# Gated GELU projection on one core: eight early units instead of six, with their first blocks loaded in sequence of columns

## The chip, the cores and the metric

The kernel runs on one core of one Trainium2 chip. A core has TensorE (matrix products, accumulated in eight PSUM banks of 128 x 512 float32), VectorE and ScalarE (which read SBUF and PSUM), GpSimd (SBUF only) and SyncE, which here issues DMAs. In the profile they are PE (PEld is its weight load), DVE, ACT, POOL and SP. The metric is the device time of one execution in microseconds (us); of several executions the median counts.

## The reference

```python
def reference(x, w_gate, w_up, w_down):
    g = jnp.einsum("bsd,df->bsf", x, w_gate)
    u = jnp.einsum("bsd,df->bsf", x, w_up)
    h = _gelu(g) * u
    return jnp.einsum("bsf,fd->bsd", h, w_down)
```

x is 2048 x 1024, w_gate and w_up are 1024 x 3584, w_down is 3584 x 1024, all bf16. `_gelu` is the tanh approximation. The output is 2048 x 1024.

## The kernel before

**Passes and units.** The 2048 rows of x are taken in two passes of 1024 (`ip`), each in two halves c = 0 and 1 of 512 rows. In SBUF, x stands transposed as `xT[c]`: 128 partitions of the contraction index, eight K blocks of 128 (four "lo", four "hi"), 512 rows. The 3584 columns of w_gate and w_up are 28 blocks of 128. A *unit* (`unit`, line 222) computes two blocks h = 0 and 1 of h = gelu(g) * u for both halves c, in a scheme of seven products instead of eight: the 2 x 2 matrix of (block, K half) times the 2 x 2 matrix of (K half, row half). Its operands are sums. `sums_t` (line 149) makes t1 to t4 out of the four quarters of x, once a pass, four 128 x 512 sums each, and `tb` as a cast. `sums_s` (line 164) makes s1 to s4 out of the four quarters of a unit's weights, two 128 x 512 sums each (gate and up), and `sa` as a cast. The products are

- P1 = a11 b11 and P2 = a12 b21, of plain bf16 data, whose sum is the result for block h = 0 and c = 0;
- s2 t2 (on top of P1), s1 t1, s3 t3, s4 tb and sa t4, of the sums in float32.

Each has eight matmuls of 128 x 128 by 128 x 512: four K blocks for gate and four for up. A unit's P1 and P2 are thus 16 matmuls in bf16, and the five others 40. P1 is copied from PSUM to SBUF by ScalarE (`snap`, line 106) before P2 is added in the same bank. Between the products ScalarE copies partial results (u2, p5), takes gelu, and VectorE adds and multiplies; the finished block goes to `hT`.

**Early units.** In the first pass the first R = 6 units have P1 and P2 done ahead of all float32 products, because those need nothing but x and the first block of the unit's weights. `early_p1`, `early_snap`, `early_p2` and `early_c11` (lines 503 to 524) do this; `seed` (line 526) later puts P1 back into PSUM. The units from R on have P1 and P2 done in `raw_products`, two units at a time, ahead of the last product of an odd unit (`ahead_of_p4`, line 621). Which blocks of columns early units take is free; `block` (line 139) says where they stand in `hT`.

**Weights.** `load_w` (line 124) loads 256 columns (rows of 512 bytes) of w_gate and of w_up, 512 KB each, so one load holds two blocks. Later units use the two blocks of one load. The early units use two loads together: units 0 and 1 take their first blocks from load 0 and their second ones from load 1, units 2 and 3 from loads 2 and 3, units 4 and 5 from loads 4 and 5. Loads 0 to 2 stand in the three buffers of `wpool`, loads 3 to 5 in the part of `hT` that is written last.

**What sets the order.** VectorE, GpSimd, SyncE and TensorE run their instructions in the order of the source. ScalarE's order comes from the framework's scheduler and departs from the source in places. Each engine works its list strictly in order and waits for semaphores. SyncE's list is the order of the loads (lines 482 to 496); load 4 alone is issued by ScalarE (line 553). The second half of x is transposed by two DMAs (line 490), the first by TensorE (`turn`, line 457) from plain loads.

**The stage in question** (lines 530 to 573): the first rows of x are turned while P1 of units 0 and 1 starts; P2 of these; P1 and P2 of units 2 and 3; the same for units 4 and 5. On VectorE stand in between t1, s1, s2 of unit 0, then t2, t3, s3, s4 and t4. GpSimd makes the sums of unit 1 (`make_s(early[1], pool)`, line 573) and then, inside each unit (`prepare`, line 603), those of the next one, with nothing ahead of them but the loads. `pool_behind` (line 179) is defined and not used: a one-element copy on GpSimd that waits for a given tile.

**After the units** the second projection (`down`, line 372) runs with a similar scheme over `hT`; the second pass follows. Neither is touched.

Of the kernel before, what the change touches and what calls it, by code (L numbers as in the profile page):

```python
# [10 lines left out]
def kernel(  # L11
# [39 lines left out]
    NKB = Dm // P  # L51
# [3 lines left out]
    N = 512  # L55
# [1 line left out]
    NPASS = S // (2 * N)  # L57
    NU = NFB // 2
    NWARM = 7
    R = 6  # L60
    SLOTS = 52
    LAG = 3
    BIG12 = (0, 2, 4)
# [47 lines left out]
    def as_f32(ap):  # L111
        return ap.rearrange("p a b -> p (a b)").bitcast(f32)

    def matmul(ps, lhs, rhs, start, stop):
        nc.tensor.matmul(  # L115
            ps, lhsT=lhs, rhs=rhs, start=start, stop=stop, skip_group_check=True
        )
# [3 lines left out]
    def new_w():  # L121
        return wpool.tile([P, 2, NKB, 2 * P], bf16, name="w")

    def load_w(n, w, k0=0, k1=NKB, queue=nc.sync):
        f0 = n * 2 * P
        for i, src in enumerate((w_gate, w_up)):
            queue.dma_start(  # L127
                out=w[:, i, k0:k1],
                in_=src[k0 * P : k1 * P, f0 : f0 + 2 * P].rearrange(
                    "(ko ki) f -> ki ko f", ki=P  # L130
                ),
            )
        return w

    def blocks_of(w, w2=None, q=0):
        pair = ((w, 0), (w, 1)) if w2 is None else ((w, q), (w2, q))
        return [[v[:, i, :, n * P : (n + 1) * P] for i in range(2)] for v, n in pair]

    def block(ip, u, h):
        return u // 2 * 4 + 2 * h + u % 2 if ip == 0 and u < R else 2 * u + h  # L140

    class Sums(dict):

# [328 lines left out]
    def transposing(xT, c, ko, r0):  # L472
# [2 lines left out]
        )  # L475

    on_dve, on_act = nc.vector.tensor_copy, nc.scalar.copy
    far = hT[:, 1, 2:14].rearrange("p j c n -> p (j c n)").rearrange(
        "p (m i k f) -> p m i k f", m=3, i=2, k=NKB
    )  # L480
    wa = {0: new_w(), 1: new_w(), 2: new_w(), 3: far[:, 0], 4: far[:, 1], 5: far[:, 2]}
    load_x(0)
    load_w(0, wa[0], 0, 2)
    load_w(0, wa[0], 2, 4)
    load_x(1)
    load_w(0, wa[0], 4, 8)
    load_w(2, wa[2])
    for half in range(2):
        ks = slice(half * KH, (half + 1) * KH)
        nc.sync.dma_start_transpose(  # L490
            out=xT[1][:, ks], in_=x2[N : 2 * N, half * N : (half + 1) * N]
        )
        if half == 0:
            load_w(1, wa[1])
    load_w(3, wa[3])
    load_w(5, wa[5])
    early = [blocks_of(wa[u // 2 * 2], wa[u // 2 * 2 + 1], u % 2) for u in range(R)]
    seen = xpool.tile([P, 1], f32, name="seen")
    E, K, C, F = odd, cc, dd, even
    s, t = sums_s(early[0], dve), sums_t(xT)  # L500
    p1s = {}

    def early_p1(u, ps, i, ks, cols=slice(0, N)):
        for k in ks:
            matmul(
                ps[i][:, cols],
                early[u][0][i][:, k, :],
                xT[0][:, k, cols],
                k == 0 and cols.start == 0,
                k == KH - 1,  # L510
            )

    def early_p2(u, ps, i, ks):
        for k in ks:
            matmul(ps[i], early[u][0][i][:, KH + k, :], xT[0][:, KH + k, :], False, k == KH - 1)

    def early_snap(u, ps):
        at = [None, None]
        if u >= 4:
            at = [as_f32(hT[:, n // 14, n % 14]) for n in (4 + 2 * u, 5 + 2 * u)]  # L520
        p1s[u] = [snap(ps[i], "p1", at[i]) for i in range(2)]

    def early_c11(u, ps):
        times(block(0, u, 0), 0, gelu(ps[0]), ps[1])

    def seed(u, e):
        for i in range(2):
            nc.scalar.copy(out=e[i], in_=p1s[u][i])  # L528

    on_queue = nc.scalar  # L530
# [50 lines left out]
    def loaded(u):  # L581
        if u not in ws:
            ws[u] = load_w(u, new_w())
        return blocks_of(ws[u])

    def raw_of(u, e):
        p1 = raw_products(e, K, xT, loaded(u))
        return lambda: finish_raw(2 * u, K, p1)

    def weights(ip, u):  # L590
        return early[u] if ip == 0 and u < R else loaded(u)

    for ip in range(NPASS):
        with tc.manual_schedule(engines={ENG.Activation}):
# [102 lines left out]
```

## Time and profile before

| | us |
|---|---|
| median of 3 runs (550.7 to 555.04) | 552.34 |
| the profiled execution | 551.14 |
| its span | 549.4 |
| TensorE busy, share of the span | 534.5, 97% |
| VectorE busy | 345.1, 63% |
| ScalarE busy | 271.0, 49% |
| GpSimd busy | 250.1, 46% |
| granted TensorE clock | 0.999 |

The span is from the first to the last instruction of the profiled execution. A line of the timeline gives the start and the time of a run of like instructions (us), the engine (SPq is SyncE's DMA issue), the source line, the operation, the tile written and those read, the shapes and the count, and in brackets how long the engine had been idle before and what ended the idle time. L115 is the helper for all matmuls, L91 and L94 those for two-operand operations on VectorE and GpSimd, L127 the weight loads. The chain of work that ended last is followed back from the last instruction, at each step to what released it; it is shown in order of time. TensorE's busy time is modelled at the ends of matmuls, so 97% does not mean that it is at its peak.

By stages (us of the span): up to 11.63 the first transposes and the P1 of units 0 and 1; to 22.33 their P2 and units 2 and 3; to 33.33 units 4 and 5; to 48.28 unit 0; then unit 1 to 57.51 and unit 2 to 66.74. DMAs move 260 GB/s from 3.60 to 33.33 and almost nothing from 34 to 46.

### The profile page before, as it was taken

The page shows a single profiled execution, that of the slowest core. Times are in us where ns is not written, and L with a number is a line of the kernel's source. Part 1 is how long each engine was busy: PE and PEld are TensorE (multiplying, and loading weights), DVE is VectorE, ACT ScalarE, POOL GpSimd, SP SyncE. Part 2 cuts the span into 40 slices and gives each one's busy share as a digit, 9 for nine tenths or more (in the row PEclk, how much of TensorE's full clock was granted, in tenths as well). Part 3 has the DMA queues.
Part 4 walks back from the last instruction along what each step waited for, and adds up shares of the span by engine and source line. Part 5 has one row for each costly group of instructions (what it writes and reads, how often), then busy time and mean ns, then how long its engine had stood idle before and what let it go on. Part 6 is the DMA issues. An engine that isn't in the chain of part 4 may idle for free.

```text
span 549.4 us, 7452 instructions
## 1 busy us (share of the span) xinstructions
PE 534.5 (97%) x2380; PEld 383.2 (70%) x2399; DVE 345.1 (63%) x520; ACT 271.0 (49%) x484; POOL 250.1 (46%) x220
## 2 busy tenths in 40 slices
PE   8878999999999999999999999999999999999997
PEld 4346787768686854888868686767768685478886
DVE  1596767667667696586874645555555548766730
ACT  3465786666675701155435564565555551114531
POOL 0369999767666310000058667676767600000000
PEclk9999999999999999999999999999999999999999
DMA  8951369394863799999937222222422039663751
GB/s 234 248 130 38 98 196 280 100 284 124 223 170 99 267 343 383 276 237 233 343 112 180 78 76 78 77 78 76 106 59 68 1 102 382 224 228 95 222 189 53
DMA packets 108520, 93.29 MB, mean 170 GB/s; under 512 B 17089, under 2 KB 93889, under 8 KB 108481
## 3 DMA queue, kind: packets, MB, share of 16 engines
q1 hardware_dynamic: 106400, 91.77, 57.3%
q10 hardware_dynamic: 2080, 1.05, 0.9%
q8 instruction: 19, 0.31, 0.2%
q14 instruction: 21, 0.16, 0.1%
HBM read 74.45 MB, written 15.20 MB: 163 GB/s over the span
## 4 chain that ended last, share of the span: by engine, by line
PE 88%; DMA 5%; DVE 3%; SPq 2%; issue 1%; ACT 0%; DVEq 0%; ACTq 0%
PE bank L115 88%; DMA raw<-in_w_down_dram 3%; DVE t L91 2%; DMA w<-in_w_up_dram 2%; SPq L127 1%; SPq L490 1%; DVE hT L91 1%; DVE s L91 0%; SPq L450 0%; ACT g L194 0%; DVE sum L91 0%; ACT st L419 0%; ACT bank L528 0%; DVEq L91 0%; SPq L340 0%
## 5 line engine op out<-in xcount | busy, mean ns | idle before, releaser
L94 POOL TENSOR_TENSOR s<-w 128x512 fp32r<-128x512 bf16 x88 | 103.2, 1190 | 169.4 <-DVE t L91 86.2
L115 PE MATMUL bank<-t,s 128*128 128x512 f32 x672 | 158.6, 391 | 4.8 <-ACT bank L528 2.3
L115 PEld LDWEIGHTS bank<-t,s 128*128 128x128 f32 x672 | 125.5, 188 | 33.9 <-POOL s L94 1.9
L115 PE MATMUL bank<-xT,w 128*128 128x512 bf16 (+1 forms) x411 | 90.2, 375 | 2.1 <-ACT p L108 1.2
L91 DVE TENSOR_TENSOR hT<-g,bank 128x512 bf16<-128x512 f32 x112 | 76.9, 688 | 22.4 <-PE bank L115 7.6
L194 ACT ACTIVATE g<-sum 128x512 f32<-128x512 f32 x78 | 49.5, 634 | 75.4 <-DVE sum L91 74.0
L108 ACT COPY p<-bank 128x512 f32<-128x512 f32 x96 | 54.3, 590 | 45.6 <-PE bank L115 45.3
L115 PEld LDWEIGHTS <-w 128*128 128x128 bf16 x424 | 40.3, 98 | 50.0 <-issue 4.4
L91 DVE TENSOR_TENSOR sum<-bank,p 128x512 f32<-128x512 f32 x36 | 24.9, 692 | 77.8 <-PE bank L115 77.8
L115 PE MATMUL bank<-q 128*128 128x512 f32 x240 | 58.9, 389 | 0.0
L115 PE MATMUL bank<-t,sa 128*128 128x512 f32 x224 | 57.6, 399 | 0.8 <-DVE sum L91 0.8
L94 POOL TENSOR_TENSOR s<-w,s 128x512 fp32r<-128x512 bf16 x48 | 56.0, 1187 | 0.0
L94 POOL TENSOR_TENSOR s<-s,w 128x512 fp32r<-128x512 f32 x48 | 55.7, 1182 | 0.0
L115 PE MATMUL bank<-tb,s 128*128 128x512 f32 x224 | 55.3, 389 | 0.0
L115 PEld LDWEIGHTS bank<-q 128*128 128x128 f32 x240 | 45.0, 188 | 9.4
L115 PEld LDWEIGHTS bank<-t,sa 128*128 128x128 f32 x224 | 42.0, 188 | 10.8 <-DVE sum L91 1.3
L115 PE MATMUL bank<-raw,hT 128*128 128x512 bf16 x218 | 48.5, 379 | 0.4
L103 ACT CAST tb<-raw 128x512 fp32r<-128x512 bf16 x28 | 17.3, 626 | 63.3 <-DMA raw<-in_w_down_dram 27.7
L115 PEld LDWEIGHTS <-hT 128*128 128x128 bf16 x256 | 24.7, 98 | 33.6 <-DMA hT<-in_w_up_dram 2.2
L115 PEld LDWEIGHTS bank<-tb,s 128*128 128x128 f32 x224 | 42.0, 188 | 8.7
L91 DVE TENSOR_TENSOR q<-hT 128x512 fp32r<-128x512 bf16 x56 | 38.4, 686 | 3.9 <-PE bank L115 3.9
L108 ACT COPY xT<-bank 128x512 f32<-128x512 f32 x56 | 31.5, 590 | 11.4 <-PE bank L115 6.2
(54 smaller groups left out, 543.5 us busy)
## 6 DMA issues: line engine op xcount, KB each, us to landing
raw<-in_w_down_dram SPq DMA_DIRECT2D x76, 256.0 KB, 4.8
q<-td SPq DMA_DIRECT2D x60, 256.0 KB, 5.0
w<-in_w_gate_dram SPq DMA_DIRECT2D x24, 512.0 KB, 5.4
w<-in_w_up_dram SPq DMA_DIRECT2D x24, 512.0 KB, 6.5
td<-m SPq DMA_DIRECT2D x12, 768.0 KB, 4.5
w<-td SPq DMA_DIRECT2D x6, 1024.0 KB, 10.3
out_dram<-st SPq DMA_DIRECT2D x32, 128.0 KB, 1.7
td<-w SPq DMA_DIRECT2D x2, 768.0 KB, 6.4
```

The source lines that it names most:

```text
L91: nc.vector.tensor_tensor(out=out, in0=a, in1=b, op=op)
L94: nc.gpsimd.tensor_tensor(out=out, in0=a, in1=b, op=op)
L103: nc.scalar.copy(out=t, in_=src)
L108: nc.scalar.copy(out=t, in_=ps)
L115: nc.tensor.matmul(ps, lhsT=lhs, rhs=rhs, start=start, stop=stop, skip_group_check=True)
L127: queue.dma_start(out=w[:, i, k0:k1], in_=src[k0 * P : k1 * P, f0 : f0 + 2 * P].rearrange("(ko ki) f -> ki ko f", ki=P),)
L194: nc.scalar.activation(g, src, ACT.Gelu_apprx_tanh)
L490: nc.sync.dma_start_transpose(out=xT[1][:, ks], in_=x2[N : 2 * N, half * N : (half + 1) * N])
```

## The change

R goes from 6 to 8. The first blocks of the eight early units are now the first eight blocks of columns: blocks 0 and 1 in `wa`, blocks 2 to 5 in `mid`, loaded with 512 columns (rows of 1 KB) in two K halves, blocks 6 and 7 in `end`. The second blocks come from loads 4 to 7: loads 4 and 5 at the start, loads 6 and 7 when `early(u)` first asks for them. `mid` and `end` stand in `hT`. All loads are on SyncE's queue, in the order x, `wa`, first half of `mid`, a transposed half of x, second half of `mid`, the other transposed half, `end`, load 4, load 5. P1 of units 2 to 5 now goes in one run, then their P2, then units 6 and 7. One of P1's two copies goes to the place in `hT` of the unit's second block. VectorE has t1 to t4 among the products of the early units and s1 to s4 behind them; `tb` is cast later; the last transposed block of x is copied by VectorE alone, and unit 0's P1 copies come earlier. A `pool_behind` on s2 of unit 0 stands ahead of GpSimd's sums of unit 1.

```diff
-    R = 6
+    R = 8
...
-    def load_w(n, w, k0=0, k1=NKB, queue=nc.sync):
+    def load_w(n, w, k0=0, k1=NKB, wide=2):
         f0 = n * 2 * P
         for i, src in enumerate((w_gate, w_up)):
-            queue.dma_start(
+            nc.sync.dma_start(
                 out=w[:, i, k0:k1],
-                in_=src[k0 * P : k1 * P, f0 : f0 + 2 * P].rearrange(
+                in_=src[k0 * P : k1 * P, f0 : f0 + wide * P].rearrange(
...
     def block(ip, u, h):
-        return u // 2 * 4 + 2 * h + u % 2 if ip == 0 and u < R else 2 * u + h
+        return u + R * h if ip == 0 and u < R else 2 * u + h
...
-    wa = {0: new_w(), 1: new_w(), 2: new_w(), 3: far[:, 0], 4: far[:, 1], 5: far[:, 2]}
+    far = hT[:, 1, 2:14].rearrange("p j c n -> p (j c n)")
+    wa, mid, end = new_w(), *[
+        v.rearrange("p (i k f) -> p i k f", i=2, k=NKB)
+        for v in (far[:, : 4 * NKB * 2 * P], far[:, 4 * NKB * 2 * P :])
+    ]
+    pairs_of = {0: new_w(), 1: new_w()}
+
+    def load_x1(half):
+        nc.sync.dma_start_transpose(
+            out=xT[1][:, half * KH : (half + 1) * KH],
+            in_=x2[N : 2 * N, half * N : (half + 1) * N],
+        )
+
     load_x(0)
-    load_w(0, wa[0], 0, 2)
-    load_w(0, wa[0], 2, 4)
+    load_w(0, wa, 0, 2)
+    load_w(0, wa, 2, 4)
     load_x(1)
-    load_w(0, wa[0], 4, 8)
-    load_w(2, wa[2])
-    for half in range(2):
-        ks = slice(half * KH, (half + 1) * KH)
-        nc.sync.dma_start_transpose(
-            out=xT[1][:, ks], in_=x2[N : 2 * N, half * N : (half + 1) * N]
-        )
-        if half == 0:
-            load_w(1, wa[1])
-    load_w(3, wa[3])
-    load_w(5, wa[5])
-    early = [blocks_of(wa[u // 2 * 2], wa[u // 2 * 2 + 1], u % 2) for u in range(R)]
+    load_w(0, wa, 4, 8)
+    load_w(1, mid, 0, KH, wide=4)
+    load_x1(0)
+    load_w(1, mid, KH, NKB, wide=4)
+    load_x1(1)
+    load_w(3, end)
+    load_w(4, pairs_of[0])
+    load_w(5, pairs_of[1])
+    first = [block_of(wa, u) for u in range(2)] + [block_of(mid, u) for u in range(4)]
+    first += [block_of(end, u) for u in range(2)]
+
+    def early(u):
+        if u // 2 not in pairs_of:
+            pairs_of[u // 2] = load_w((R + u) // 2, new_w())
+        return [first[u], block_of(pairs_of[u // 2], u % 2)]
...
     def early_snap(u, ps):
-        at = [None, None]
-        if u >= 4:
-            at = [as_f32(hT[:, n // 14, n % 14]) for n in (4 + 2 * u, 5 + 2 * u)]
+        n = block(0, u, 1)
+        at = [as_f32(hT[:, n // NJ, n % NJ]), None]
         p1s[u] = [snap(ps[i], "p1", at[i]) for i in range(2)]
...
+        early_snap(0, E)
         turn(bank[6], 1, 0, (on_dve,))
         early_p1(*pairs[2], range(2, KH))
-        turn(bank[7], 1, 1, (on_dve, on_act))
+        turn(bank[7], 1, 1, (on_dve,))
         early_p1(*pairs[3], range(2, KH))
-        early_snap(0, E)
         early_snap(1, K)
...
-        load_w(4, wa[4], queue=on_queue)
-        for us in (((2, C), (3, F)), ((4, E), (5, K))):
-            for u, ps in us:
-                for i in range(2):
-                    early_p1(u, ps, i, range(KH))
-                early_snap(u, ps)
-            if us[0][0] == 2:
-                t.make("t1")
-                s.make("s1", "s2")
-            else:
-                t.make("t2")
-            for u, ps in us:
-                for i in range(2):
-                    early_p2(u, ps, i, range(KH))
-                early_c11(u, ps)
-                if u == 4:
-                    t.make("t3", "tb")
+        four = ((2, C), (3, F), (4, E), (5, K))
+        for u, ps in four:
+            for i in range(2):
+                early_p1(u, ps, i, range(KH))
+            early_snap(u, ps)
+        t.make("t1", "t2")
+        for u, ps in four:
+            for i in range(2):
+                early_p2(u, ps, i, range(KH))
+            early_c11(u, ps)
+            if u == 3:
+                t.make("t3")
+            if u == 4:
+                t.make("t4")
         seed(0, F)
+        two = ((6, E), (7, K))
+        for u, ps in two:
+            for i in range(2):
+                early_p1(u, ps, i, range(KH))
+            early_snap(u, ps)
+        t.make("tb")
+        s.make("s1", "s2")
+        pool_behind(s["s2"][-1][:, 0])
         s.make("s3", "s4", "sa")
-        t.make("t4")
-        nxt = {"s": make_s(early[1], pool)}
+        for u, ps in two:
+            for i in range(2):
+                early_p2(u, ps, i, range(KH))
+            early_c11(u, ps)
+        nxt = {"s": make_s(early(1), pool)}
```

C, F, E and K are names for pairs of PSUM banks; units 0, 4 and 6 use E, units 1, 5 and 7 use K, unit 2 uses C and unit 3 F. The later unit 0 begins in F and goes on in E.

More of the change, by code (lines that the diff above doesn't have):

```diff
@@ L133, in load_w, with block_of @@
         return w
-    def blocks_of(w, w2=None, q=0):
-        pair = ((w, 0), (w, 1)) if w2 is None else ((w, q), (w2, q))
-        return [[v[:, i, :, n * P : (n + 1) * P] for i in range(2)] for v, n in pair]
+    def block_of(w, n):
+        return [w[:, i, :, n * P : (n + 1) * P] for i in range(2)]
     def block(ip, u, h):
-        return u // 2 * 4 + 2 * h + u % 2 if ip == 0 and u < R else 2 * u + h
+        return u + R * h if ip == 0 and u < R else 2 * u + h
     class Sums(dict):
@@ L477 @@
     on_dve, on_act = nc.vector.tensor_copy, nc.scalar.copy
-    far = hT[:, 1, 2:14].rearrange("p j c n -> p (j c n)").rearrange(
-        "p (m i k f) -> p m i k f", m=3, i=2, k=NKB
-    )
-    wa = {0: new_w(), 1: new_w(), 2: new_w(), 3: far[:, 0], 4: far[:, 1], 5: far[:, 2]}
+    far = hT[:, 1, 2:14].rearrange("p j c n -> p (j c n)")
[9 more added lines that the diff above has]
+        )
     load_x(0)
-    load_w(0, wa[0], 0, 2)
-    load_w(0, wa[0], 2, 4)
+    load_w(0, wa, 0, 2)
+    load_w(0, wa, 2, 4)
     load_x(1)
-    load_w(0, wa[0], 4, 8)
-    load_w(2, wa[2])
-    for half in range(2):
-        ks = slice(half * KH, (half + 1) * KH)
-        nc.sync.dma_start_transpose(
-            out=xT[1][:, ks], in_=x2[N : 2 * N, half * N : (half + 1) * N]
-        )
-        if half == 0:
-            load_w(1, wa[1])
-    load_w(3, wa[3])
-    load_w(5, wa[5])
-    early = [blocks_of(wa[u // 2 * 2], wa[u // 2 * 2 + 1], u % 2) for u in range(R)]
+    load_w(0, wa, 4, 8)
[12 more added lines that the diff above has]
+        return [first[u], block_of(pairs_of[u // 2], u % 2)]
     seen = xpool.tile([P, 1], f32, name="seen")
     E, K, C, F = odd, cc, dd, even
-    s, t = sums_s(early[0], dve), sums_t(xT)
+    s, t = sums_s(early(0), dve), sums_t(xT)
     p1s = {}
@@ L506, in early_p1 @@
                 ps[i][:, cols],
-                early[u][0][i][:, k, :],
+                first[u][i][:, k, :],
                 xT[0][:, k, cols],
@@ L514, in early_p2 @@
         for k in ks:
-            matmul(ps[i], early[u][0][i][:, KH + k, :], xT[0][:, KH + k, :], False, k == KH - 1)
+            matmul(ps[i], first[u][i][:, KH + k, :], xT[0][:, KH + k, :], False, k == KH - 1)
     def early_snap(u, ps):
-        at = [None, None]
-        if u >= 4:
-            at = [as_f32(hT[:, n // 14, n % 14]) for n in (4 + 2 * u, 5 + 2 * u)]
+        n = block(0, u, 1)
+        at = [as_f32(hT[:, n // NJ, n % NJ]), None]
         p1s[u] = [snap(ps[i], "p1", at[i]) for i in range(2)]
@@ L528, in seed @@
             nc.scalar.copy(out=e[i], in_=p1s[u][i])
-    on_queue = nc.scalar
     with tc.manual_schedule(engines={ENG.Activation}):
@@ L583, in loaded @@
             ws[u] = load_w(u, new_w())
-        return blocks_of(ws[u])
+        return [block_of(ws[u], n) for n in range(2)]
     def raw_of(u, e):
@@ L590, in weights @@
     def weights(ip, u):
-        return early[u] if ip == 0 and u < R else loaded(u)
+        return early(u) if ip == 0 and u < R else loaded(u)
     for ip in range(NPASS):
```

## The prediction

> **What bounds the kernel now.** I read the busy shares first (PE 97%), then the chain that ended last, in order of time, because 97% hides where the rest lies. From 48.28 us on it is TensorE nearly alone:
>
> ```profile
> 48.28 44.47 PE bank L115 x192
> 92.75 0.07 issue
> 92.82 25.01 PE bank L115 x111
> ```
>
> The reader is to see that after 48.28 only gaps of some 0.07 us are left. What can be won lies before, or in fewer instructions later. So the timeline of TensorE up to 60 us comes next:
>
> ```profile
> 11.63 10.70 PE L115 MATMUL bank<-xT,w 128*128 128x512 bf16 x47 [1.19 <-ACT p L108]
> 23.24 1.04 PE L115 MATMUL bank<-xT,hT 128*128 128x512 bf16 x4 [0.91 <-DMA hT<-in_w_gate_dram]
> 25.97 6.22 PE L115 MATMUL bank<-xT,hT 128*128 128x512 bf16 x28 [1.69 <-DMA hT<-in_w_up_dram]
> 33.33 1.18 PE L115 MATMUL bank<-t,s 128*128 128x512 f32 x3 [1.14 <-ACT bank L528]
> 35.58 3.24 PE L115 MATMUL bank<-t,s 128*128 128x512 f32 x13 [1.07 <-DVE t L91]
> 40.25 2.08 PE L115 MATMUL bank<-t,s 128*128 128x512 f32 x8 [1.44 <-DVE s L91]
> ...
> 48.28 5.71 PE L115 MATMUL bank<-t,s 128*128 128x512 f32 x24 [1.19 <-ACT bank L528]
> ```
>
> Unit 0 runs from 33.33 to 48.28, 14.95 us; unit 1, the same 40 products, from 48.28 to 57.51, 9.23 us. Unit 0 loses 5.7 us to sums that come late, and 2.6 us more (0.91 and 1.69) go to the late load of load 4. Why the sums are late: VectorE's and GpSimd's timelines.
>
> ```profile
> 16.32 2.50 DVE L91 TENSOR_TENSOR t<-xT,xT 128x512 fp32r<-128x512 bf16 x4
> ...
> 29.25 6.27 DVE L91 TENSOR_TENSOR t<-xT,t 128x512 fp32r<-128x512 bf16 x4
> ...
> 41.84 2.49 DVE L91 TENSOR_TENSOR t<-xT,t 128x512 fp32r<-128x512 bf16 x4
> ```
>
> ```profile
> 29.12 2.72 POOL L94 TENSOR_TENSOR s<-w 128x512 fp32r<-128x512 bf16 x2
> ...
> 41.45 3.89 POOL L94 TENSOR_TENSOR s<-hT 128x512 fp32r<-128x512 bf16 x1 [4.90 <-PE bank L115]
> ```
>
> A sum on VectorE takes 0.62 us with GpSimd idle (2.50/4), 1.57 us while GpSimd makes its own (6.27/4). At 41.45 it is GpSimd's that waits, 3.89 us.
>
> **The credit.** The two further early units take their P1 and P2 ahead, so two fewer blocks of 16 products come later. From 92.82 on, a period of two units and two such blocks takes 25.08 us; two units without take 18.46. One period becomes two bare units: 6.62 us less. The end therefore moves by (48.28 + 6.62) - T1 = 54.90 - T1, where T1 is the start of unit 1 after the change. Everything hangs on T1.
>
> **The walk to T1.** Rows used: bf16 products 0.217 us each (28 in 6.22 and, one record missing, 48 in 10.70, tails of 0.2 taken off), so a block of eight 1.74; 0.62 for a sum, 0.60 for a gated product on VectorE, 0.59 for a copy or gelu, 0.2 to 0.25 from an end to its reader.
>
> *Blocks 0 and 1.* P1's copies go partly to other places at the same rows' price. ScalarE's copies of P1 move ahead of the last transposed block, whose copy goes whole to VectorE (0.69 as at 9.11). P2 starts at 10.8 (10.05 + 0.69) instead of 11.63. It ends at 14.3.
>
> *P1 of units 2 to 5*, 32 products, 14.3 to 21.25. Their weights stand where load 2 stood: issued at 5.87 and 6.46, landed after 7.0 and 8.1 us, 12.9 and 14.6; hidden. Whether 1-KB rows are quicker, the stage shows poorly (x with such rows 301 GB/s in 2 to 4 us, 512-byte rows 290 to 300 in 26 to 32): nothing either way.
>
> *The queue.* SyncE's issues before:
>
> ```profile
> 9.51 4.70 SPq L490 DMA_TRANSPOSE xT<-in_x_dram  x1
> ...
> 15.50 8.51 SPq L490 DMA_TRANSPOSE xT<-in_x_dram  x1
> ```
>
> They landed 6.7 and 11.6 us after their issue, at 16.2 and 27.1. The second shared the engines with load 4 from ScalarE's queue (1 MB from 15.03). After the change nothing is on that queue, and 5.24 MB go in order up to the end of the second transposed half; by windows of 2 us before, 5.36 MB had moved at 22, 4.78 at 20, 6.17 at 26, 7.35 at 30, 8.40 at 34. I take 22 for its landing, 19.8 for the second K half ahead of it, 26.4 for load 3, 30 for load 4, 34 for load 5. Ends for the 22: 21.4 (the 1.57 MB behind the first half, landed at 16.2, at 301 GB/s) and 30.8 (both issues at 8.51, see the rivals). The windows are nearest, being the same bytes through the same engines. Loads 3 (`end`), 4 and 5 are queued behind that issue; they are wanted at 28.2, 32.5 and about 46. ScalarE loses the two issues of load 4 (0.42 and 1.73 us); hidden, since the copies behind them had 2.40 us idle.
>
> *P2 of units 2 to 5*, 21.25 to 28.2: the K half at 19.8 is hidden by P1; at 24.3 (where load 1's second half landed from this place) it costs 2.3.
>
> *VectorE's row*, in its new order: t1 16.3 to 18.8, t2 from 22 to 24.5, products of units 2 and 3 (unit 3's P2 ends at 24.7, gelu by 25.55) to 26.2, t3 to 28.7, unit 4 to 29.35, t4 to 31.85, unit 5 to 32.45. So VectorE, not TensorE, is late: unit 7's up half uses unit 5's bank and starts at 32.5, ending at 33.4. With P2 of units 6 and 7 (3.47) TensorE is through at 36.9: T0, the start of unit 0. s1 and s2 are ready at 34.9, hidden by those products. If the second transposed half lands after 22.5, T0 moves with it, us for us.
>
> *The gate on GpSimd.* It starts at 34.9 instead of 20.28. Behind it wait unit 1's eight sums, 9.2 us at the 1.15 of 55 to 95 us, 13.2 at 1.65: done by 44 to 48, and TensorE wants s2 first. The added one-element copy costs between 0.10 (the 128x1 memset) and 1.15 us, hidden likewise. Afterwards GpSimd takes 9.2 us a unit as TensorE does, with some 5 us in hand (unit 2's s2 by 52.6, wanted at 58.0). Loads 6 and 7 now come during units, where 40 to 46 us shows the queue empty.
>
> *ScalarE's row.* In the built program of the changed kernel its order here is: copies of P1 of units 6 and 7, four casts tb, then unit 0's two u2 copies, two casts sa, and only then the gelus of units 6 and 7. But unit 0's second product goes into unit 6's banks. In unit 1 of before the u2 copies begin 1.25 and 2.16 us after the unit's start (49.53, 50.44); then 0.59, 1.14 for sa, 0.6 for gelu: the bank is free at T0 + 4.5 where TensorE wants it at T0 + 1.85. A new stall of 2.65 us; lower end 0, if the wait is not where I read it, upper 3.3 with the second gelu.
>
> T1 = 36.9 + 9.23 + 2.65 = 48.8. The gain is 54.90 - 48.8 = 6.1 us: 545.0 on the profiled execution's 551.14. The median of the runs shown is 1.2 higher, 552.34, so the forecast in its terms is **546.2**.
>
> [...] After s2 VectorE still has s3 and s4, while GpSimd starts. By row 41.45 GpSimd waits out such a run, and s4 ends at 37.4. [...]
>
> [...] The issue at 15.03 put 1 MB beside the transposed half, which then landed 11.6 us after its issue against 6.7; the sum goes by the rows.
>
> **Rivals.**
> - *No stall in unit 0* (ScalarE's order costs nothing, loads on time). For it: the stall stands in no row of before, and ScalarE is idle for about two us ahead of it. Against: the order stands in the program. Gain 8.8, 543.6.
> - *The second transposed half still lands late.* For it: 8.51 us of issue in one row; against: load 4 no longer beside it. At 25 to 27.1 T1 is 51.3 to 53.4, the gain 3.6 to 1.5: 548.7 to 550.8, no change.
> - *Slower: one queue in one line.* If both transposing issues take 8.51 us (9.5 to 18.0; K half to 19.2; 19.2 to 27.7) and the landing follows 3.1 us after, as at 27.1, the second lands at 30.8, T0 is 45.2, T1 57.1: 2.2 slower, 554.5. It turns to a loss when that half lands after 28.6. A loss over 1% needs 34.1.
> - *The change gives no bare units.* If GpSimd at 1.65 us a sum (20 to 36 us) takes 13.2 a unit against 9.23, six units lose 24 us less the 5 in hand, against the 6.1 gained: 565, slower. Against: from 48 on VectorE's sums have one operand in PSUM and GpSimd's row is 1.15.
>
> **How the numbers follow.** What can be told from no change here is about 1%, 5.5 us: faster means under 546.8, a T1 under 49.4. Forecast (545 to 548, with up to 24 for the landing) 0.47, of which 0.31 fall under 546.8; no stall 0.16; late half 0.28; queue 0.05 and GpSimd 0.04. Faster 0.47, same 0.45 (0.16 + 0.28 and a part of the queue's), slower 0.08. The range takes in the no-stall case and the late half: 543 to 551.
>
> **What would show it.** T2 to T8 at 9.23 us apart and one period of 25 us fewer; VectorE's t2, t3 and t4 at 0.62; TensorE waiting some 2.6 us for a gelu inside unit 0 and about 1 us for unit 5's product; GpSimd's first sum at about 35. I am wrong if t2 starts after 24, if TensorE waits for `end` or load 4, or if GpSimd ends a wait of TensorE after unit 1.

## The result and the profile after

| | before | after |
|---|---|---|
| median of 6 executions each (us) | 552.12 | 545.1 |
| lowest and highest (us) | 550.45, 555.92 | 544.05, 545.99 |
| profiled execution, its span (us) | 551.14, 549.4 | 544.05, 542.3 |
| TensorE busy | 534.5, 97% | 534.3, 99% |

The ratio of the times is 0.9863, interval 0.9824 to 0.9902: 7 us faster, inside the range of 543 to 551 and 1.1 us under the forecast of 546.2. TensorE does the same amount of work in a shorter span, so the whole gain is idle time of the first stage. Its timeline after, with the start, the time of the run of matmuls and, in brackets, the idle time before it and what ended that:

```profile
14.45 16.57 PE L115 MATMUL bank<-xT,hT 128*128 128x512 bf16 x76
31.89 4.48 PE L115 MATMUL bank<-xT,hT 128*128 128x512 bf16 x20 [0.88 <-DVE hT L91]
36.02 2.21 PE L115 MATMUL bank<-t,s 128*128 128x512 f32 x8
40.44 3.92 PE L115 MATMUL bank<-t,s 128*128 128x512 f32 x16 [2.21 <-ACT g L193]
44.20 1.98 PE L115 MATMUL bank<-tb,s 128*128 128x512 f32 x8
46.01 1.97 PE L115 MATMUL bank<-t,sa 128*128 128x512 f32 x8
47.85 5.72 PE L115 MATMUL bank<-t,s 128*128 128x512 f32 x24
```

T0, the start of unit 0, is 36.02; T1, the start of unit 1, is 47.85. Between 14 and 36 us one wait is left, 0.88 us for the product of unit 5; inside unit 0 one, 2.21 us, for a gelu. With one of 0.44 us at 11.00, for a copy of x, that makes three waits, 3.5 us together. From 11.63 on the timeline of before has eight, 9.5 us together: the seven that the prediction shows, and one inside unit 0, for a sum that VectorE makes only behind t4:

```profile
44.98 2.11 PE L115 MATMUL bank<-t,sa 128*128 128x512 f32 x8 [0.84 <-DVE sum L91]
```

By the credit, the end should move by 54.90 - 47.85 = 7.05 us; the span moved by 7.1. The chain that ended last, in order of time (start, us, what), shows where the 2.21 us come from:

```profile
38.27 0.59 ACT xT L108
38.85 1.03 ACT sa L103 x2
39.89 0.51 ACT g L193
40.40 0.04 issue
40.44 498.51 PE bank L115 x2216
```

ScalarE makes unit 0's second u2 copy (`xT`, L108), then two casts `sa`, and only then the gelu that frees unit 6's bank. From 40.44 to the last copies of the output the chain is TensorE alone. The chain's earlier part goes back through VectorE's list to the second transposed half of x, issued at 15.03 and landed at 22.04. SyncE's timeline, its issues alone:

```profile
8.19 5.63 SPq L485 DMA_TRANSPOSE xT<-in_x_dram  x1
...
15.03 4.95 SPq L485 DMA_TRANSPOSE xT<-in_x_dram  x1
```

The halves landed 7.6 and 7.0 us after their issue began; before, it was 6.7 and 11.6. VectorE's timeline then has the sums t2, t3, t4 and s3, s4:

```profile
22.13 2.50 DVE L91 TENSOR_TENSOR t<-xT,t 128x512 fp32r<-128x512 bf16 x4 [3.71 <-DMA xT<-in_x_dram]
25.74 2.49 DVE L91 TENSOR_TENSOR t<-xT 128x512 fp32r<-128x512 bf16 x4
28.75 2.49 DVE L91 TENSOR_TENSOR t<-xT,t 128x512 fp32r<-128x512 bf16 x4
31.16 0.68 DVE L91 TENSOR_TENSOR hT<-g,bank 128x512 bf16<-128x512 f32 x1
...
35.37 1.29 DVE L91 TENSOR_TENSOR s<-w,s 128x512 fp32r<-128x512 bf16 x2
```

Every sum takes 0.62 us (2.49/4), where t2 of before took 1.57. The 0.68 at 31.16 is the product of unit 5 for which TensorE waits: t4 stands ahead of it. GpSimd's timeline begins late, as the gate wants it:

```profile
34.31 2.39 POOL L179 COPY seen<-s 128x1 f32<-128x1 f32 x1 [33.01 <-DVE s L91]
36.66 2.27 POOL L94 TENSOR_TENSOR s<-w 128x512 fp32r<-128x512 bf16 x2
```

The one-element copy takes 2.39 us: it ends when VectorE's last sum does (35.37 + 1.29 = 36.66).

### The profile page after: what moved, and what is told of

Same layout as the page of the kernel before. It is cut to its first block, busy times and chain, and to the rows that moved or that the text cites. A ratio compares the mean times of both kernels' runs of the same rounds, so it can differ in the third digit from the quotient of the medians.

```text
span 542.3 us, 7464 instructions
## 1 busy us (share of the span) xinstructions
PE 534.3 (99%) x2399; PEld 383.2 (71%) x2399; DVE 336.5 (62%) x516; ACT 273.3 (50%) x487; POOL 246.1 (45%) x221
## 4 chain that ended last, share of the span: by engine, by line
PE 93%; SPq 3%; DVE 2%; DMA 1%; ACT 1%; issue 0%; DVEq 0%
PE bank L115 93%; DVE t L91 1%; DMA xT<-in_x_dram 1%; SPq L127 1%; SPq L485 1%; DVE hT L91 0%; SPq L449 0%; ACT sa L103 0%; ACT xT L108 0%; ACT st L418 0%; ACT g L193 0%; DVEq L91 0%
## 5 line engine op out<-in xcount | busy, mean ns | idle before, releaser
L94 POOL TENSOR_TENSOR s<-w 128x512 fp32r<-128x512 bf16 x92 | 106.5, 1177 | 138.2 <-PE bank L115 100.5
L193 ACT ACTIVATE g<-sum 128x512 f32<-128x512 f32 x76 | 48.2, 634 | 70.1 <-DVE sum L91 66.9
L115 PE MATMUL bank<-xT,w 128*128 128x512 bf16 (+1 forms) x360 | 78.6, 375 | 0.7 <-DVE xT L466 0.7
L108 ACT COPY p<-bank 128x512 f32<-128x512 f32 x92 | 52.7, 589 | 45.3 <-PE bank L115 45.3
L91 DVE TENSOR_TENSOR sum<-bank,p 128x512 f32<-128x512 f32 x34 | 23.5, 692 | 75.9 <-PE bank L115 75.9
L115 PEld LDWEIGHTS <-w 128*128 128x128 bf16 x360 | 34.1, 98 | 41.7 <-issue 2.6
L115 PEld LDWEIGHTS <-hT 128*128 128x128 bf16 x320 | 31.1, 98 | 38.9 <-issue 1.7
L94 POOL TENSOR_TENSOR s<-w,s 128x512 fp32r<-128x512 bf16 x40 | 46.0, 1171 | 0.0
L94 POOL TENSOR_TENSOR s<-s,w 128x512 fp32r<-128x512 f32 x40 | 45.7, 1163 | 0.0
L108 ACT COPY xT<-bank 128x512 f32<-128x512 f32 x56 | 31.7, 590 | 10.2 <-PE bank L115 8.6
```

Source lines behind the costliest of these rows:

```text
L91: nc.vector.tensor_tensor(out=out, in0=a, in1=b, op=op)
L94: nc.gpsimd.tensor_tensor(out=out, in0=a, in1=b, op=op)
L108: nc.scalar.copy(out=t, in_=ps)
L115: nc.tensor.matmul(ps, lhsT=lhs, rhs=rhs, start=start, stop=stop, skip_group_check=True)
L193: nc.scalar.activation(g, src, ACT.Gelu_apprx_tanh)
```

## Experiments

**The stand-in.** No kernel of this section uses the transposing DMA. All stand on a copy of the changed kernel (one, b0, on a copy of the kernel before) in which the 18 transposing loads of x are plain ones of the same bytes, places and waits; the x of the second row half and of the second pass is thus not transposed, and the values of the output are others.

```diff
     def load_x1(half):
-        nc.sync.dma_start_transpose(
-            out=xT[1][:, half * KH : (half + 1) * KH],
-            in_=x2[N : 2 * N, half * N : (half + 1) * N],
+        nc.sync.dma_start(
+            out=xT[1][:, half * KH : (half + 1) * KH].rearrange("p k (t f) -> p (k t) f", f=P),
+            in_=x2[:, half * P : (half + 1) * P].rearrange("(m p) f -> p m f", p=P),
         )
```

(The 16 loads of the second pass are edited in the same way. The plain loads have rows of 256 bytes.)

The runs came in three groups, each on another chip: c0, b0, g3 and g4; g1, g5, g6 and h1; g2, g7, h2 and i1. The kernel before, run beside each group, had medians of 552.16, 552.02 and 551.18 us. A difference of under 1 us between medians of two groups is therefore not counted as shown; times within one profile are read for that.

> A stand-in for the changed kernel, to which the next ones are compared: the 18 transposing transfers of x are replaced by plain ones of the same size (rows of 256 bytes), so the values of x's later halves are not those of the transposed x; every other instruction is as in the changed kernel. If a plain transfer moves and issues at the pace of the others, the second half of x lands by its bytes at 20 to 22 instead of 22.04, VectorE's products of units 2 and 3 then bind, unit 0 starts within 0.7 us of 36.02 and the time is 543 to 545. If the transposing form itself was slow (5.63 and 4.95 us of issue), all loads behind land up to 4 us earlier, with the same end.

Measured: 545.86 us (544.39 to 546.68), ratio to before 0.9859 (0.9813 to 0.9904); the changed kernel has 0.9863. The profiled execution took 544.39; t2 starts at 22.43, T0 is 36.40, the gelu's stall 2.21, T1 48.20. Each is within 0.4 us of the changed kernel, so the stand-in serves. The half landed later than the 20 to 22 expected, and the median lies over the 543 to 545 expected: three of the four executions have a granted clock of 0.996 or 0.997 and took 545.80 to 546.68; the fourth, at 1.000, is the profiled one. One difference: the issue of the plain half takes 0.51 us, but the load behind it, `end`, takes 4.79. So the long issue is not the transposing form's own: a plain load at that place of the queue takes nearly as long (4.95 in the changed kernel).

**The kernel before with plain loads** (b0: the same edit).

> The same stand-in for the kernel before: its 18 transposing transfers replaced by plain ones of the same size, values of x's later halves left wrong, all else as it was. Theory (load 4 beside the second transposed half, and GpSimd's sums beside VectorE's, made the stage late): loads come 1 to 3 us earlier, the collisions stay, unit 1 starts at 45 to 48, the time is 548 to 552. Rival (the transposing transfers alone held the queue, 8.51 us for the second, and made before late): with plain ones unit 1 starts before 44 and the time is under 547.

Measured: 554.08 us (552.13 to 556.81), ratio 1.0033 (1.0002 to 1.0064). The gain of the change is there without transposing loads (554.08 to 545.86), so it is not their form that held the kernel before up. But the time lies over the 548 to 552 of the theory too, and unit 1 starts at 51.36, not at 45 to 48: the loads did not come earlier. TensorE's timeline:

```profile
23.78 1.04 PE L115 MATMUL bank<-xT,hT 128*128 128x512 bf16 x4 [1.55 <-DMA hT<-in_w_gate_dram]
26.83 9.10 PE L115 MATMUL bank<-xT,hT 128*128 128x512 bf16 x28 [2.01 <-DMA hT<-in_w_up_dram]
```

The waits for load 4 are there again, 1.55 and 2.01 us where before has 0.91 and 1.69. The 28 matmuls behind them took 9.10 us, against 6.22 in the profile of before: from 25.9 to 32.7 us the granted clock was 0.50. More on that below. A wait of 3.43 us for a sum of VectorE inside unit 0 comes on top.

**The gate on GpSimd.** g4 takes it away:

```diff
         s.make("s1", "s2")
-        pool_behind(s["s2"][-1][:, 0])
         s.make("s3", "s4", "sa")
```

> The stand-in without the one-element copy that holds GpSimd back. GpSimd then starts on unit 1's sums when load 4 has landed, some 26 to 30 us, instead of at 36.7. Theory (the two engines slow each other, as at 29.25 of the kernel before): t4, s1 and s2 on VectorE take about 1.57 us a sum instead of 0.62, 4 to 8 us more in all, unit 0 starts 3 to 6 us later and the time is 3 to 6 us over the stand-in's. Rival (VectorE's row runs through and GpSimd is the one that waits, as at 41.45 of before and at 34.31 of after): VectorE stays at 0.62 and the time within 1 us of the stand-in's.

Measured: 550.83 us (548.33 to 552.48), ratio 0.9954 (0.9924 to 0.9983), so 5.0 us over the stand-in. GpSimd starts at 28.03, when load 4 lands. VectorE's timeline:

```profile
28.83 4.77 DVE L91 TENSOR_TENSOR t<-xT,t 128x512 fp32r<-128x512 bf16 x4
33.52 0.67 DVE L91 TENSOR_TENSOR hT<-g,bank 128x512 bf16<-128x512 f32 x1
34.12 2.60 DVE L91 TENSOR_TENSOR s<-w 128x512 fp32r<-128x512 bf16 x2
36.64 3.22 DVE L91 TENSOR_TENSOR s<-s,w 128x512 fp32r<-128x512 f32 x2
```

t4 takes 4.77 instead of 2.49, so the product of unit 5 is ready some 2 us later, and T0 is 38.37 instead of 36.40. That is the collision, 2.0 us, less than the 3 to 6 expected: s1 and s2 slow down as well, but most of that is hidden. The time met the expected 3 to 6 us only with the help of what follows. T1 is later by more, by 53.59 - 48.20 = 5.4; another 0.5 of it is a slower first product, with a wait of 0.27 for one of the sums. The timeline of TensorE shows the rest:

```profile
34.24 4.48 PE L115 MATMUL bank<-xT,hT 128*128 128x512 bf16 x20 [3.24 <-DVE hT L91]
...
43.31 6.79 PE L115 MATMUL bank<-t,s 128*128 128x512 f32 x16 [2.21 <-ACT g L193]
```

Sixteen matmuls of unit 0 take 6.79 us where the stand-in has 3.92. The stage in windows of 1 us gives the reason: window, its length, busy time and instructions of TensorE, weight load, VectorE, ScalarE and GpSimd, then the granted clock, the DMAs' share and GB/s:

```profile
41.00:42.00 1.00, 0.10 (x1) 0.00 (x0) 1.00 (x3) 0.86 (x2) 0.00 (x0) 1.00 0.00 0
42.00:43.00 1.00, 0.00 (x0) 0.00 (x0) 1.00 (x3) 1.00 (x3) 0.00 (x0) 0.82 0.00 0
43.00:44.00 1.00, 0.69 (x2) 0.60 (x3) 0.95 (x3) 0.74 (x2) 0.00 (x0) 0.50 0.00 0
...
48.00:49.00 1.00, 1.00 (x3) 0.74 (x3) 0.09 (x1) 0.80 (x2) 0.99 (x2) 0.50 0.00 0
49.00:50.00 1.00, 1.00 (x5) 0.78 (x4) 0.60 (x1) 0.37 (x1) 1.00 (x1) 0.76 0.00 0
```

The clock falls to one half during the idle gap of 2.21 us and comes back only near 49.5 (the shares 0.82 and 0.76 put it at 42.6 to 49.5, 6.8 us). The same gap in the profile of the stand-in had no such spell. That made the clock a suspect of its own.

**The clock.** h1 is g4 with matmuls of a constant, into a bank free at the time, in TensorE's two gaps:

```diff
+        def fill(n):
+            for _ in range(n):
+                nc.tensor.matmul(bank[4], lhsT=warm[:, :P], rhs=warm, start=True, stop=True)
+
         for u, ps in two:
             for i in range(2):
+                if u == 7 and i == 1:
+                    fill(14)
                 early_p1(u, ps, i, range(KH))
...
                 def aside():
+                    if ip == 0 and u == 0:
+                        fill(10)
```

> The stand-in without the gate on GpSimd (550.83 us, granted clock 0.990 to 0.997, a spell of clock 0.50 from 42.8 to 48.8 in its profile), with 14 and 10 added matmuls of constants into a free bank ahead of unit 7's up half and of unit 0's second product, where TensorE waited 3.24 and 2.21 us. Their results are overwritten. Theory (the half clock follows TensorE's idle gaps): the clock is 1.000 in all executions, they lie within 0.5 us of each other and the time is 547 to 548. Rival (the half clock has another cause, the engines or transfers at work beside it): spells stay and the time is 550 to 551.5.

Measured: 547.51 us (546.88 to 548.30), ratio 0.9908 (0.9869 to 0.9947), the clock 1.000 in all eight executions. TensorE's timeline:

```profile
40.89 2.36 PE L583 MATMUL bank<-const-bfloat16-1.0 128*128 128x512 bf16 x10
43.26 3.92 PE L115 MATMUL bank<-t,s 128*128 128x512 f32 x16
```

The gap is full, the product behind it starts at the same time as in g4 (43.26 and 43.31), waits for the same gelu, and takes 3.92. So 24 matmuls more made the kernel 3.3 us faster: in g4 the gap of 2.21 us brought 2.87 us more in the 16 matmuls behind it, which is more than its own length. The eight executions were expected within 0.5 us of each other. The spread that is left, 1.4 us, was not traced. h2 does the same with the stand-in itself, whose one larger gap is the gelu's:

```diff
                 def aside():
+                    if ip == 0 and u == 0:
+                        for _ in range(10):
+                            nc.tensor.matmul(bank[4], lhsT=warm[:, :P], rhs=warm, start=True, stop=True)
```

> The stand-in with ten added matmuls of constants into a free bank, ahead of unit 0's second product, where TensorE waits 2.21 us; their results are overwritten (x's later halves by plain transfers). The stand-in's executions were 544.39 at clock 1.000 and 545.80 to 546.68 at 0.996 to 0.997. Theory (the half clock follows the gap): clock 1.000 in all, 544.2 to 544.7 in all. Rival (it comes from elsewhere): the same spread, up to 546.7.

Measured: 544.41 us (543.77 to 544.60), ratio 0.9872 (0.9843 to 0.9902). The stand-in's own executions are 544.39 at a clock of 1.000 and 545.80 to 546.68 at 0.996 and 0.997; filled, they all lie at 0.999 or above and below 544.7. That puts the upper part of the stand-in's spread down to that gap, on four executions against four. In g2, which ran beside h2 and keeps the gap, two of four have 0.996 and 0.997. The changed kernel's two longest executions, 545.88 and 545.99, have 0.997 as well, which points to the same gap, though it was not filled there. Compared with both gaps filled, leaving the gate out costs some 3 us (547.51 against 544.41).

**The stall of the gelu.** In g1 units 6 and 7 take the pairs C and K instead of E and K, so that unit 0's second product finds its banks free whatever ScalarE does first:

```diff
-        two = ((6, E), (7, K))
+        two = ((6, C), (7, K))
```

> The stand-in (x's later halves by plain transfers, their values not the transposed x) with units 6 and 7 in the bank pairs C and K instead of E and K; t4 stays ahead of unit 5's product. Theory (the stall in unit 0 is ScalarE's order and the shared pair): TensorE's wait of 2.21 us for a gelu goes and the 0.81 for unit 5's product stays; unit 1 starts 1.7 to 2.2 us before the stand-in's 48.20, the time is 541.8 to 542.7. Rival (the two waits hang together, one edit frees both or neither): 541.1 as with both edits, or 544.4.

Measured: 542.22 us (542.06 to 542.49), ratio 0.9812 (0.9752 to 0.9872). The wait for the gelu is gone, and T1 is 46.03 instead of 48.20. T0 is 36.02 instead of 36.40, as VectorE's list ran 0.3 to 0.4 us sooner from t2 on (22.14 against 22.43), which is none of the edit's doing. Unit 0 takes 10.01 us instead of 11.80, so the edit itself brings 1.8: a smaller wait comes ahead of unit 1, 0.54 us for the copy that puts P1 back (L540). The time is 2.2 us under the stand-in's profiled 544.39, and the spread is 0.43 us instead of 2.29: no execution has a clock below 0.999.

**The place of t4.** g2 puts t4 behind the product of unit 5:

```diff
-            if u == 4:
+            if u == 5:
                 t.make("t4")
```

> The stand-in with t4 behind unit 5's gated product alone; units 6 and 7 stay in E and K (x's later halves by plain transfers). Theory (VectorE's list in order holds unit 5's product back): TensorE's wait of 0.81 us goes, the one of 2.21 us for a gelu stays, the profiled execution is 0.8 to 1.2 us under the stand-in's 544.39, so 543.2 to 543.6, with clock 1.000 or up to 1.5 us more where it is below. Rival (s1 and s2, no earlier than before, take its place): 544.4.

Measured: 544.17 us (543.09 to 544.60), ratio 0.9867 (0.983 to 0.9904). TensorE's wait of 0.81 for the product of unit 5 is gone, the gelu's 2.21 stays, and T0 is 35.70 instead of 36.40, T1 47.52. At a clock of 1.000 the pair is 543.09 against 544.39.

**Both** (g3: the edits of g1 and g2).

> The stand-in with two edits: units 6 and 7 in the bank pairs C and K, so unit 0's second product writes no pair that unit 6's gelu still has to read; and t4 behind unit 5's gated product instead of ahead of it. Theory (the waits of 2.21 us for a gelu and 0.88 us for unit 5's product have these two causes): both waits go, unit 1 starts about 3.1 us earlier than in the stand-in and the time is 3 us under the stand-in's. Rival (sums or GpSimd take their place): less than 1.5 us, with new waits of TensorE for s after 36 us.

Measured: 541.09 us (541.04 to 541.20), ratio 0.9768 (0.9731 to 0.9805). TensorE's timeline:

```profile
14.40 20.88 PE L115 MATMUL bank<-xT,hT 128*128 128x512 bf16 x94
34.93 5.82 PE L115 MATMUL bank<-t,s 128*128 128x512 f32 x24
...
44.91 5.71 PE L115 MATMUL bank<-t,s 128*128 128x512 f32 x24 [0.54 <-ACT bank L540]
```

From 14.40 to the end of unit 0 no wait of TensorE shows; the 0.54 us ahead of unit 1 stay. T1 is 44.91, 3.29 before the stand-in's; the profiled time is 3.30 lower, the median 4.8, and the spread 0.16 us. The same two edits on the changed kernel with its transposing loads were not tried; that they carry over is likely, since neither touches a load, but not shown.

**Load 4 on ScalarE's queue**, as before:

```diff
     load_w(3, end)
-    load_w(4, pairs_of[0])
     load_w(5, pairs_of[1])
...
         early_c11(1, K)
+        load_w(4, pairs_of[0], queue=nc.scalar)
         four = ((2, C), (3, F), (4, E), (5, K))
```

> The stand-in with load 4 issued by ScalarE behind the gelus of units 0 and 1, where before had its load 4, and taken out of SyncE's queue; x's later halves are by plain transfers. Theory (its 1 MB then moves beside the second half of x): that half lands at 24 to 27 instead of 22.4, t2 starts then, unit 0 starts 1.5 to 4.5 us later, the time is 546 to 549. Rival (a second queue changes only where the issue time is spent): the half lands within 0.7 us of 22.4 and the time stays within 1 us of 544.4.

Measured: 549.26 us (548.48 to 550.29), ratio 0.9938 (0.9914 to 0.9961). VectorE's timeline:

```profile
26.24 2.50 DVE L91 TENSOR_TENSOR t<-xT,t 128x512 fp32r<-128x512 bf16 x4 [7.68 <-DMA xT<-in_x_dram]
...
35.26 0.68 DVE L91 TENSOR_TENSOR hT<-g,bank 128x512 bf16<-128x512 f32 x1
```

t2 started at 22.43 in the stand-in, so the half is 3.8 us later, as the theory has it; the time is 0.3 over the theory's range. T0 is 40.53 (4.1 later) and T1 52.35 (4.15 later), the profiled time 4.1 higher. Nearly all of it is VectorE's list, moved as a whole: the product of unit 5, at 31.54 in the stand-in, is at 35.26, 3.7 later. The clock plays a part too: TensorE waited 3.90 us for a product, and the 28 matmuls behind that took 7.89 us, against 6.22 for 28 in the profile of before. But that is mostly hidden, as the last 20 of them need the product of unit 5, ready at 35.94, and took 4.13 us behind it in the stand-in: 40.1 at full clock, so some 0.4 of the 4.1 is the clock's.

**The rows of 512 bytes.** g5 loads `mid` as eight pieces of 256 KB with rows of 512 bytes, in the same order of K halves (`load_mid` loads two column halves, each of 256 columns as `load_w` does):

```diff
-    load_w(1, mid, 0, KH, wide=4)
+    load_mid(0, KH)
     load_x1(0)
-    load_w(1, mid, KH, NKB, wide=4)
+    load_mid(KH, NKB)
     load_x1(1)
```

> The stand-in with blocks 2 to 5 loaded with rows of 512 bytes, in eight transfers of 256 KB instead of four of 512 KB; K halves and order stay, x's later halves are by plain transfers as there. Theory (the bytes in order decide, not the rows): the second half of x lands at 22 to 23 and the time stays within 0.7 us of the stand-in's lowest, 544.4. Rival (the 1-KB rows moved the bytes faster: 334 and 345 GB/s at 8 to 12 us of after against 271 and 296 of before): the second half of x lands at 23 to 24.5, unit 0 starts 0.7 to 2 us later and the time is 545 to 547.

Measured: 547.10 us (546.42 to 547.58), ratio 0.9899 (0.9848 to 0.995), 1.2 over the stand-in's median, as the rival has it. Two windows show it, first of the stand-in, then of g5 (the last column is GB/s):

```profile
10.00:12.00 2.00, 1.56 (x13) 0.82 (x14) 0.69 (x1) 0.95 (x2) 0.00 (x0) 1.00 1.09 368
```

```profile
10.00:12.00 2.00, 1.56 (x9) 0.52 (x7) 0.69 (x1) 1.69 (x3) 0.00 (x0) 1.00 1.17 298
```

While the first K half of `mid` loads, the rate is 298 GB/s instead of 368. Added up over such windows, 5.09 MB had moved by 20 us in the stand-in (5.19 in g1 and 5.18 in g4, which load `mid` alike) and 4.86 in g5. t2 starts at 23.53 instead of 22.43, T0 is 37.41 instead of 36.40. The size of the pieces is changed along with the rows, and the two were not told apart.

**The K halves.** i1 loads `mid` whole, ahead of both halves of x:

```diff
-    load_w(1, mid, 0, KH, wide=4)
+    load_w(1, mid, wide=4)
     load_x1(0)
-    load_w(1, mid, KH, NKB, wide=4)
     load_x1(1)
```

> The stand-in with mid loaded whole, two transfers of 1 MB with 1-KB rows, ahead of both later parts of x (which are by plain transfers), instead of in K halves around the first of them. Theory (VectorE waits for the second part of x alone, and the bytes ahead of it are the same): t1 starts 2 to 4 us later, at 18 to 20, t2 still at 22 to 23, and the time stays within 0.7 us of 544.4. Rival (the K halves are needed: with them the first part of x and t1 come early enough): t2 is pushed past 23, and the time rises by over 1 us.

Measured: 547.04 us (546.41 to 547.40), ratio 0.9921 (0.9891 to 0.9951): a miss of the theory, 2.6 above the 544.4 of the stand-in's profiled execution. The rival's sign came: t2 starts at 23.36, not at 22.43. TensorE's timeline has a wait besides that neither named:

```profile
17.12 15.71 PE L115 MATMUL bank<-xT,hT 128*128 128x512 bf16 x72 [1.40 <-DMA hT<-in_w_up_dram]
```

P1 of unit 2 wants four K blocks of gate and four of up by 15.7 us. Loaded whole, 1 MB of gate comes ahead of the first block of up. The wait puts P2 of unit 3 off, and VectorE's list behind t2 waits for it:

```profile
26.90 0.69 DVE L91 TENSOR_TENSOR hT<-g,bank 128x512 bf16<-128x512 f32 x1 [0.44 <-PE bank L115]
```

T0 is 37.77, 1.37 later: 0.93 for the later t2 and 0.44 for this product. In this execution a clock spell follows in unit 0's gap (16 matmuls in 5.53 us); the three others, at a clock of 1.000, took 546.41 to 547.27, and where they lost the rest is open.

**Six units.** g7 leaves units 6 and 7 out of the early ones and keeps all else (order, K halves, gate):

```diff
-    R = 8
+    R = 6
...
-    load_w(3, end)
-    load_w(4, pairs_of[0])
-    load_w(5, pairs_of[1])
+    load_w(3, pairs_of[0])
+    load_w(4, pairs_of[1])
...
-        for u, ps in two:
-            for i in range(2):
-                early_p1(u, ps, i, range(KH))
-            early_snap(u, ps)
...
-        for u, ps in two:
-            for i in range(2):
-                early_p2(u, ps, i, range(KH))
-            early_c11(u, ps)
```

> The stand-in with six early units, all else as changed (x's later halves by plain transfers): blocks 0 to 5 come first, loads 3, 4 and 5 hold the second blocks. Theory (the two further early units are worth the time in which they cover VectorE's list): TensorE is through with P2 of unit 5 at about 28 and s2 is ready at 34.3, so it waits some 6 us for s; unit 1 starts at about 43.6, but the 6.62 us of two units' P1 and P2 come back later: 546.4, and up to 3 us more where the long gap is followed by half clock. Rival (order and loads bring nothing by themselves, R = 8 is the whole gain): 551 to 552.

Measured: 548.23 us (547.62 to 548.76), ratio 0.9925 (0.9889 to 0.9961). TensorE's timeline:

```profile
33.82 7.22 PE L115 MATMUL bank<-t,s 128*128 128x512 f32 x24 [5.40 <-DVE s L91]
```

VectorE has no sooner made s1 and s2 (t1 to t4 stand ahead of them), so TensorE waits 5.40 us, and the 24 matmuls behind the gap take 7.22 instead of 5.72. The P1 and P2 of units 6 and 7, 6.9 us of matmuls that depend on neither, fill most of this gap in the changed kernel. They also bring the gelu's stall: here unit 0 has none, and T1 is 44.54 against 48.20, so that 3.0 us of the 6.62 are left. On the stand-ins' medians the two units bring 2.4 us of the 8.2 (554.08 to 545.86), order, loads and gate 5.8; by the ratios to the kernel before beside each group it is 3.6 of 9.6. The split holds for this sequence alone, and it has the clock in it: eight units in the old order were not run, and neither was the new order of VectorE's sums by itself.

## Why the prediction was right, point by point

| step | predicted | measured (after) |
|---|---|---|
| P2 of units 0 and 1 starts | 10.8 | 11.00 |
| second K half landed | 19.8 | 18.9 and 20.3 (gate, up) |
| second transposed half landed | 22 | 22.04 |
| product of unit 5 done | 32.45 | 31.8 |
| TensorE's wait for it | about 1 | 0.88 |
| T0 | 36.9 | 36.02 |
| added copy on GpSimd | 0.10 to 1.15, hidden | 2.39, hidden |
| s4 done | 37.4 by the row | 36.66 |
| stall in unit 0, start to start | 2.65 | 2.58 (TensorE idle for 2.21) |
| T1 | 48.8 | 47.85 |
| gain, profiled executions | 6.1 | 7.09 |

- **The credit and its formula held**: 54.90 - T1 gave the span to 0.05 us, units 1 to 7 start 9.25 to 9.27 apart, and from 40.44 on the chain is TensorE's own up to the last copies. P1 and P2 of two later units come three times in the first pass (110.78, 135.88 and 160.96 us), where before has them four times.
- **T0 was 0.9 us too late**: the product of unit 5 came 0.6 us sooner, and the matmuls behind it took 4.13 us where the sum has 4.4. The product was late in the sum because it let unit 3's gelu wait for all of P2 (24.7 us); the gelu reads the gate's bank alone and started at 24.14, so t3 began at 25.74 and not at 26.2. The step of the second landing, on which everything hung, was right.
- **The stall was read in the right place, and its price was right to 0.1 us.** The sum counts from start to start: 4.5 us from T0 to the second product, less the 1.85 that the first one takes. Measured, that is 4.42 us (36.02 to 40.44), and T1 - T0 is 11.83, 2.58 over the 9.25 of unit 1. The 2.21 of the timeline is TensorE's idle time alone and begins behind the last matmul's tail. So the whole error of T1 is that of T0. g1 shows by taking the bank away that the shared pair is the cause.
- **The gate was counted as hidden, and is.** What it is worth was not worked out: without it the kernel is 5.0 us slower (g4), some 3 of it with the gaps filled on both sides (h1, h2), the rest by the clock.
- **VectorE and GpSimd at once.** The added copy's 2.39 us lie over four sums of VectorE (1.29 us for two at 34.16 and at 35.37), and s4 ended at 36.66, near the 37.4 that the prediction took from row 41.45 of before. In g4, where GpSimd's sums had begun ahead of t4 (28.03 and 28.83), both slow down: t4 took 1.19 us a sum instead of 0.62, GpSimd 1.58 beside it instead of the 1.14 that it has behind VectorE's sums in the changed kernel (2.27 for two at 36.66). Why one case goes one way and the other another, no run shows.
- **"1-KB rows: nothing either way" was wrong** by some 1.2 us (g5). The window of 2 to 4 us that the prediction took for 1-KB rows has the first 512-byte loads of `wa`, issued from 1.75 on, in it as well, so it could not tell. Rows and size of the pieces are not told apart in g5 either.
- **The rivals.** No stall: its condition was not met; where the edit of g1 makes it so, 1.8 us come of the 2.65, since a wait of 0.54 takes its place. Late half: not met; g6 brings it about, and its 549.26 lies in the 548.7 to 550.8. One queue in line: the issues took 5.63 and 4.95 us, not 8.51. GpSimd as the bound: in the whole profile no wait of TensorE is put down to it, and the chain does not pass through it.
- **The second queue.** The prediction put the late landing of before down to the 1 MB of load 4 beside the half, and g6 bears that out: the same 1 MB from ScalarE's queue put t2, which waits for the half, from 22.43 to 26.24. With load 4 off that queue the half landed at 22.04, where before has 27.1.
- **The median.** 1.2 us were added for the distance of the profiled execution from the median; after, that distance is 1.05. What makes it was not known then. The spells of half clock below are a part of it; but the three executions at a clock of 1.000 alone took 544.05 to 544.76, so the profiled one was also the fastest of the six.

## What to carry to other kernels

Walk the list of each engine row by row in its built order, ScalarE's too: the end of the new stage, the wait and its place came out of four lists and one landing. Work without dependencies, placed where another engine is late, is worth the wait that it covers, less the waits that it brings, and not its own time: two units more brought 2.4 us of 8.2 by the medians, and the orders and the gate the rest. And a stage with short gaps on TensorE is worth closing even by less than the gaps: two small edits of bank and place removed 3.0 us of waits, left one of 0.5 in their place and took 4.8 off the stand-in's median, the clock's share among them.

## What the runs showed of the hardware

**The granted clock after short gaps.** In the profiles of b0, g4, g5, g6, g7 and i1 a gap of TensorE of 2.0 to 5.4 us is followed, or from its middle on accompanied, by a spell at a clock of 0.50. Worked out from windows of 1 us as for g4, the spells last 6.8 us in b0 and g4 and 3.4 in the four others; the matmuls in them take 1.5 to 2.9 us longer, part of which can be hidden, as in g6. By the mean clocks they come in some executions of a kernel and not in others (the stand-in has 1.000 once, 0.996 or 0.997 three times), and the mean clock of an execution sorts the times: of the executions of before that ran beside the experiments, those at 0.999 and above took 549.4 to 552.1 us, those between 0.987 and 0.991 took 555.0 to 557.8. Where the larger gaps are filled or gone (h1, h2, g1, g3), it is 0.999 or 1.000 in every execution. A gap of 2.21 us was enough in g4, g5 and i1; the same gap in the profiles of the changed kernel, the stand-in, g2 and g6 has no spell after it. What decides between the two, and between 3.4 and 6.8 us, no run shows.

**Long issues.** With several loads issued and not landed, single issues of SyncE take 4.4 to 4.8 us for plain loads (c0) and 4.95 to 5.63 for transposing ones (after), against 0.45 to 0.47 for each of the first eight loads (after). Issues of 0.5 us stand between them, and why some take so long was not looked into.

**A one-element copy of GpSimd** took 2.39 us beside four back-to-back sums of VectorE in the changed kernel and 2.38 in the stand-in, and ended when the last of them did (36.70 and 36.66; 37.08 and 37.04).
